# HGRN2 attention and a Serf feed-forward layer: causal masks of seven chunks on ScalarE and GpSimd, a mask before the state's products, and stages of two turns at other slots

## The chip, the cores and the metric

The kernel runs on one NeuronCore of a Trainium2 chip. Its engines work side by side, each with its own in-order queue: TensorE (PE, with its weight loads listed as PEld) does matrix products into PSUM, VectorE (DVE) and ScalarE (ACT) do elementwise work on SBUF and PSUM, GpSimd (POOL) does elementwise work on SBUF, and SyncE (SP) issues nearly all of the DMAs. Semaphores order work between engines. The metric is the device time of one execution in microseconds, as the median of several runs.

## The reference

There are 4 batches, 8 heads, 768 time steps and a head size of 48. The first part is a gated linear recurrence per head, the second a feed-forward layer with the activation h·erf(softplus(h)):

```python
f = 1.0 / (1.0 + np.exp(-f_logit))
for t in range(S):
    state = f[:, :, t, :, None] * state + np.einsum('bhd,bhe->bhde', k[:, :, t], v[:, :, t])
    y[:, :, t] = np.einsum('bhd,bhde->bhe', q[:, :, t], state)
...
x = y.transpose(0, 2, 1, 3).reshape(B * S, H * D)      # 3072 x 384
h = x @ w_in                                           # 384 x 2048
sp = np.maximum(h, 0.0) + np.log1p(np.exp(-np.abs(h)))
out = (h * erf(sp)) @ w_out                            # 2048 x 384
```

## The kernel before

The 3072 rows are cut into 24 chunks of 128 time steps, numbered g = 0 to 23, six to a batch (c = g mod 6). Two chunks make a block of 256 rows; there are twelve blocks.

**Attention, four stages for each chunk.** The recurrence is done in chunks: within a chunk through a masked matrix of scores, across chunks through a state.

- `stage_d(g)`: a matmul with the triangular matrix `tri` sums the logarithms of the decays down the chunk (`ps_d`, L358). ScalarE takes exp of both signs (`dp`, `kd`, L361 and L364). For g >= 3 four small DMAs on SP put the last row of `dp`, the chunk's total decay, into `Tall` (L367). VectorE multiplies q and k by them (`qd`, `kd`, L371 and L375).
- `stage_t(g)`: eight transposes of `qd` and `kd` (`ps_t`, L385), copied out of PSUM as `qT` and `kT` (L391, L393, L395).
- `stage_s(g)`: eight matmuls give the scores `sc` (L414), 128 keys by 8 heads by 128 queries, and VectorE multiplies them by `tri` into `A` (L419): the causal mask. Ahead of the scores stands `state(g)`: eight products `dS` (L433), then four VectorE instructions (`Sn`, `Mbd`, L446 and L449; two L442 in a batch's first chunk) that add the old state and multiply by `Tall`.
- `stage_y(g)`: the products of `A` with v and of `qT` with the state of the chunk before (`y`, L146), which ScalarE copies to `xT` (L462).

`ps_d`, `ps_t`, `dS` and `y` share two PSUM buffers in rotation (`ps_at`), so each of them waits until the one before the last has been read. The scores have one buffer of their own (`ps_sc`); `A` has one in SBUF.

**Feed-forward.** `hidden` computes h for a block in four groups of 12 matmuls (L515), each evicted by ScalarE (L522) from one of two PSUM buffers. `activate` approximates the activation with an Exp, three Tanh and VectorE products (L152, L155, L160, L487, L489), one step at a time. `prepare` clamps the logits of a block on VectorE (L335) and takes Exp and Ln on ScalarE (L339, L340); Exp with Ln and Tanh lie in different tables, so that a change between them is an ACT_TABLE_LOAD. The last product runs through `project_first` for block 0 (L598) and from then on through `project`, which needs seven partial products of half size instead of eight (L645). For it `sum_w` on GpSimd and `sum_h` on VectorE form sums of the weights and of h (L543), and `plus` adds the seven results into the rows of the output in `scratch` (L653, first a copy L661).

**Weights.** w_in and w_out come as 64-bit numbers, in eight pieces each (p0 to p15). Every piece is rounded to 32 bits by one ScalarE pass (L285) and six VectorE passes (L287, L291, L296, L300, L305, L310), at the rate of the counter `due`. A group of `hidden` in the first turn needs its pieces of w_in before it runs.

**Order.** All of it is a schedule written by hand: under `manual_schedule` each engine runs its instructions in the order in which the program emits them. After the first three chunks come turns `it`. A turn runs through slots s, one matmul of the feed-forward part each; at the slots in the list `at` the stages in `todo` are emitted. In turn 0 (96 slots) `at` is written out; in turn 1 (48 slots) it is computed. `prepare(2)` is emitted at slot 17 of turn 0, later ones 14 slots before the `stage_d` that needs them. At each slot the weights' steps come first, then the stage, then `prepare`, then a step of the activation. DMAs are issued by SP in the same order.

Of the kernel before, what the change touches and what calls it, by code (L numbers as in the profile page):

```python
# [45 lines left out]
ALU = mybir.AluOpType  # L46
# [21 lines left out]
P = 128  # L68
# [3 lines left out]
def kernel(  # L72
# [10 lines left out]
    nc = tc.nc  # L83
    B, H, S, D = q.shape
# [8 lines left out]
    NCH = S // P  # L93
# [12 lines left out]
    def fixed(name, shape, dtype=FP32, pool=const):  # L106
        return pool.tile(shape, dtype, name=name)
# [82 lines left out]

    NS, NA = 3, 3
    S_WORDS = NS * NA * FG // 2 * P
    scratch = fixed("scratch", [P, S_WORDS + 7 * DH], pool=fix)
    sums_sb = scratch[:, 0:S_WORDS].rearrange("p (b n j t) -> p b n j t", b=NS, n=NA, j=FG // 2)
    rows_sb = scratch[:, S_WORDS:].rearrange("p (n c) -> p n c", n=7)

    def w_sums(gi):
        return wT[:, gi, :].rearrange("p (n j c) -> p n j c", n=NT, j=FG // 2)
# [197 lines left out]

    def stage_s(g):
        b, c = divmod(g, NCH)
        qT, kT = qTs[g], kTs.pop(g)
        if g in totals:  # L400

            pairs = dps[g % 2][:].rearrange("t (a r) d -> t a (r d)", r=2)
            for a in range(HP):
                nc.tensor.matmul(
                    totals[g][:, a : a + 1], lhsT=pairs[:, a, :], rhs=ident[:, P - 1 : P],
                    start=True, stop=True,
                )
            nc.vector.tensor_copy(out=Tall[:, g, :], in_=totals.pop(g))
        if c < NCH - 1:
            state(g, c)  # L410
        sc = ps_sc.tile([P, 2, HP, P], FP32, name="sc", tag="sc")
        for a in range(HP):
            for r in range(2):
                nc.tensor.matmul(  # L414
                    sc[:, r, a, :], lhsT=kT[rows(r), a, :], rhs=qT[rows(r), a, :],
                    start=True, stop=True,
                )
        A = work1.tile([P, 2, HP, P], FP32, name="A", tag="A")
        nc.vector.tensor_tensor(  # L419
            out=A[:].rearrange("s r a t -> s (r a) t"),  # L420
            in0=sc[:].rearrange("s r a t -> s (r a) t"),
            in1=tri[:].unsqueeze(1).broadcast_to((P, H, P)),
            op=ALU.mult,
        )
        As[g] = A

    def state(g, c):
        dS = ps_at.tile([P, HP, D], FP32, name="dS", tag="at")
# [185 lines left out]
    def project(blk):  # L614


        ops = [ps_moe.tile([P, 2, 512], FP32, name="ops", tag="moe") for _ in range(2)]
        end = blk == n_blocks - 1
        ops.append(ps_sc.tile([P, 2, 512], FP32, name="ops", tag="sc") if end else ops[1])
        place = {n: ops[i][:, j, k * DH : (k + 1) * DH] for n, (i, j, k) in {  # L620
            1: (0, 0, 0), 2: (0, 1, 0), 6: (0, 1, 1), 5: (1, 0, 0), 7: (1, 0, 1), 3: (2, 1, 0), 4: (2, 1, 1),
        }.items()}
        first = [1, 2, 5, 3]

        def pair(n):
            i, j = {2: (0, 1), 5: (1, 0), 3: (2, 1)}[n]
            return ops[i][:, j, 0 : 2 * DH].rearrange("p (n c) -> p n c", n=2)

        def products(gis, ns):
            for gi in gis:  # L630
                gr = groups[blk, gi]
                while gr["sums"] is None:
                    sum_step()
                a11, a12, a21, a22 = blocks(gr["h"])
                w = w_out_sb[:, FG * gi : FG * (gi + 1), :]
                s, t = gr["sums"], w_sums(gi)
                for j in range(2):
                    w1, w2 = w[:, j, :], w[:, 2 + j, :]
                    for n in ns:
                        x, y = {  # L640
                            1: (a11, w1[:, 0:DH]), 2: (a12, w2[:, 0:DH]), 3: (s[2], w2[:, DH:]),
                            4: (a22, t[:, 3, j, :]), 5: (s[0], t[:, 0, j, :]),
                            6: (s[1], t[:, 1, j, :]), 7: (a21, t[:, 2, j, :]),
                        }[n]
                        nc.tensor.matmul(  # L645
                            place[n], lhsT=x[:, j, :], rhs=y,
                            start=(gi == 0 and j == 0 and n in first),
                            stop=(gi == n_g - 1 and j == 1), skip_group_check=True,
                        )
                        yield  # L650

        def plus(out, x, y):
            nc.vector.tensor_tensor(out=out, in0=x, in1=y, op=ALU.add)  # L653

        o = rows_sb
        yield from products((0, 1), (1, 2, 6))
        yield from products((0,), (5, 7, 3, 4))
        to_sum.appendleft(sum_h(groups[blk, 3]))
        yield from products((1,), (5, 7, 3, 4))
        yield from products((2, 3), (1, 2, 6))  # L660
        nc.scalar.copy(out=o[:, 3, :], in_=place[1])  # L661

        plus(o[:, 0:5:4, :], o[:, 3:4, :].broadcast_to((P, 2, DH)), pair(2))
        def fives():

            plus(o[:, 5:7, :], o[:, 4:5, :].broadcast_to((P, 2, DH)), pair(5))

        yield from products((2, 3), (5, 7))
        if end:

            fives()
            plus(o[:, 3, :], o[:, 5, :], place[7])
        yield from products((2, 3), (3, 4))
        if not end:
            fives()
        plus(o[:, 1:3, :], o[:, 5:7, :], pair(3))
        if not end:
            plus(o[:, 3, :], o[:, 5, :], place[7])
        store(blk)

    def chain(*gens):
# [38 lines left out]
    with tc.manual_schedule():  # L720
# [118 lines left out]
        for it in range(n_blocks):  # L839
            gen, n = slots(it)  # L840
            if it == 0:
                todo = [(stage_d, 3), (stage_t, 3), (stage_s, 3), (stage_y, 3), (stage_d, 4), (stage_t, 4),
                        (stage_d, 5), (stage_s, 4), (stage_t, 5), (stage_y, 4)] + stages(2)[4:]
                at = [3, 10, 15, 22, 28, 36, 42, 47, 56, 74, 77, 82, 87, 93]
            else:
                todo = stages(it + 2) if it + 2 < n_blocks else []
                at = [int(3 + (n - 13) / max(1, len(todo)) * i) for i in range(len(todo))]
            if it + 3 < n_blocks:
                prepare_at = at[todo.index((stage_d, (it + 3) * CPB))] - 14
            at, todo = deque(at), deque(todo)  # L850
            for s, _ in enumerate(gen):
                due += (1 if s < 42 else 0.6 if s < 72 else 0.3) if it == 0 else 0.42 if it == 1 else 0.6
                while due >= 1:
                    weights_step()
                    due -= 1
                if s % 6 == 3:
                    load_more()
                if at and s == at[0]:
                    at.popleft()
                    f, g = todo.popleft()  # L860
                    f(g)
                    if f is stage_y:
                        load_to(g + LOOK)
                if it == 0 and s == 17:
                    prepare(2, 0, CPB)
                if it == 0 and s == 9:
                    load_f(6)
                    load_f(7)
                if s == n // 2 and it + 4 < n_blocks:
                    for j in range(CPB):  # L870
                        load_f((it + 4) * CPB + j)
                if it + 3 < n_blocks and s == prepare_at:
                    prepare(it + 3, 0, CPB)
                if it < 2:
                    step = s % 12 == 6 and (it or s >= 24)
                elif it == 2:
                    step = s % 5 in (1, 3)
                else:
                    step = s % 9 in (2, 6)
                if step:  # L880
                    act_step()
                if it == 2:
                    if s == n - 6:
                        to_sum.extend(sum_h(groups[1, gi]) for gi in range(NS))
                    sum_step()
                elif it > 2:
                    if s == n_o and it < n_blocks - 1:
                        to_sum.extend(sum_h(groups[it - 1, gi]) for gi in range(NS))
                    if it == n_blocks - 1 and s % n_o == 40 and s < 2 * n_o:
                        blk = n_blocks - 2 + s // n_o  # L890
                        to_sum.extend(sum_h(groups[blk, gi]) for gi in range(NS))
                    if s < n_o or s % 3 == 0 or it == n_blocks - 1:
                        sum_step()
                if it == n_blocks - 2 and s in (5, 40):
                    next(check)
            assert not todo
# [214 lines left out]
```

## Time and profile before

| what | value |
|---|---|
| median of 3 runs | 629.69 us (629.64 to 629.79) |
| profiled execution, its own time | 629.11 us |
| its span in the profile | 627.4 us |
| TensorE busy | 605.7 us (97%) |
| VectorE busy | 428.1 us (68%) |
| ScalarE busy | 351.8 us (56%) |
| GpSimd busy | 25.6 us (4%) |
| mean granted TensorE clock | 0.992 |

"Span" is the time from the first to the last instruction of one profiled execution. A busy time is the sum of an engine's instructions in it, without those that only branch, wait or issue DMAs. In lists of groups, "idle before" is the engine's idle time ahead of a group, with the instruction that ended most of it. The granted clock is the share of full speed at which TensorE was allowed to run. A timeline has the start in microseconds from the span's beginning, the duration, the engine, the line of the kernel, the operation, the tile written and the tiles read.

### The profile page before, as it was taken

The page shows a single profiled execution, that of the slowest core. Times are in us where ns is not written, and L with a number is a line of the kernel's source. Part 1 is how long each engine was busy: PE and PEld are TensorE (multiplying, and loading weights), DVE is VectorE, ACT ScalarE, POOL GpSimd, SP SyncE. Part 2 cuts the span into 40 slices and gives each one's busy share as a digit, 9 for nine tenths or more (in the row PEclk, how much of TensorE's full clock was granted, in tenths as well). Part 3 has the DMA queues.
Part 4 walks back from the last instruction along what each step waited for, and adds up shares of the span by engine and source line. Part 5 has one row for each costly group of instructions (what it writes and reads, how often), then busy time and mean ns, then how long its engine had stood idle before and what let it go on. Part 6 is the DMA issues. An engine that isn't in the chain of part 4 may idle for free.

```text
span 627.4 us, 11233 instructions
## 1 busy us (share of the span) xinstructions
PE 605.7 (97%) x4727; PEld 536.8 (86%) x4727; DVE 428.1 (68%) x651; ACT 351.8 (56%) x419; POOL 25.6 (4%) x24
## 2 busy tenths in 40 slices
PE   8896899899999999999999999999999999999996
PEld 7775788788668889889889989989989989989995
DVE  4898997755899576667566674684594764756751
ACT  5344655658763666665855856756747446556300
POOL 0000000000491000000000000000000000000000
PEclk9997999999999999999999999999999999999999
DMA  9999623311211211311221131031000000000000
GB/s 197 248 268 256 192 75 64 64 32 21 51 38 27 63 40 25 71 31 26 48 56 25 27 77 25 14 83 31 16 26 1 3 26 0 15 13 0 26 26 30
DMA packets 120633, 37.02 MB, mean 59 GB/s; under 512 B 112384, under 2 KB 115456, under 8 KB 120576
## 3 DMA queue, kind: packets, MB, share of 16 engines
q1 hardware_dynamic: 118496, 35.84, 24.6%
q8 instruction: 39, 0.64, 0.4%
q10 hardware_dynamic: 2080, 0.39, 0.4%
q14 instruction: 18, 0.15, 0.1%
HBM read 31.46 MB, written 4.72 MB: 58 GB/s over the span
## 4 chain that ended last, share of the span: by engine, by line
PE 80%; DVE 9%; ACT 6%; DMA 2%; issue 1%; SPq 1%; POOL 0%; DVEq 0%; POOLq 0%; ACTq 0%
PE hps L515 34%; PE ops L645 31%; PE y L146 5%; PE sc L414 3%; PE ps_t L385 3%; PE ps_d L358 2%; ACT x L155 1%; DVE e L160 1%; DMA Tall<-dp 1%; PE dS L433 1%; DVE scratch L543 1%; DVE A L419 1%; DMA lt<-in_f_logit_dram 1%; PE busy L348 1%; ACT e L152 1%
## 5 line engine op out<-in xcount | busy, mean ns | idle before, releaser
L515 PE MATMUL hps<-xT,w_in_sb 128*128 128x256 f32 x1152 | 262.0, 383 | 1.2 <-ACT xT L462 1.1
L515 PEld LDWEIGHTS hps<-xT,w_in_sb 128*128 128x128 f32 x1152 | 215.9, 191 | 35.4 <-issue 3.0
L160 DVE SCALAR_TENSOR_TENSOR e<-x,e 128x1024 f32<-128x1024 f32 x96 | 120.9, 1259 | 26.5 <-ACT x L155 26.4
L155 ACT ACTIVATE x<-Hg,serf_bias 128x1024 f32<-128x1024 f32 x88 | 97.7, 1142 | 0.1
L645 PE MATMUL ops<-wT,Hg 128*128 128x192 f32 x352 | 86.9, 329 | 0.0
L152 ACT ACTIVATE e<-Hg 128x1024 f32<-128x1024 f32 x44 | 46.6, 1059 | 63.1 <-DVE Hg L489 62.8
L522 ACT COPY Hg<-hps 128x1024 f32<-128x1024 f32 x44 | 44.4, 1010 | 62.5 <-PE hps L515 62.5
L489 DVE TENSOR_TENSOR Hg<-Hg,e 128x1024 f32<-128x1024 f32 x44 | 54.2, 1232 | 32.3 <-ACT e L487 32.3
L645 PE MATMUL ops<-wT,scratch 128*128 128x192 f32 x320 | 75.2, 327 | 0.7 <-DVE scratch L543 0.7
L645 PE MATMUL ops<-w_out_sb,Hg 128*128 128x192 f32 x352 | 74.4, 328 | 0.0
L645 PEld LDWEIGHTS ops<-wT,Hg 128*128 128x128 f32 x352 | 61.8, 190 | 2.7 <-issue 0.2
L645 PEld LDWEIGHTS ops<-w_out_sb,Hg 128*128 128x128 f32 x352 | 60.1, 190 | 3.7 <-issue 1.2
L653 DVE TENSOR_TENSOR scratch<-scratch,ops 128x384 f32<-128x384 f32 (+1 forms) x44 | 21.3, 502 | 53.2 <-ACT scratch L661 44.3
L645 PEld LDWEIGHTS ops<-wT,scratch 128*128 128x128 f32 x320 | 55.9, 190 | 1.0 <-POOL wT L543 1.0
L487 ACT ACTIVATE e<-e 128x1024 f32<-128x1024 f32 x48 | 50.5, 1051 | 6.2 <-DVE e L160 6.2
L371 DVE TENSOR_TENSOR qd<-qn,dp 128x384 f32<-128x384 f32 x24 | 13.4, 558 | 50.4 <-ACT dp L361 50.4
L146 PE MATMUL y<-A,vt 128*32 128x128 f32 x768 | 36.5, 283 | 7.7 <-DVE A L419 6.0
L146 PEld LDWEIGHTS y<-A,vt 128*32 128x32 f32 x768 | 28.1, 111 | 14.8 <-DVE A L419 5.4
L645 PE MATMUL ops<-w_out_sb,scratch 128*128 128x192 f32 x160 | 39.1, 327 | 0.0
L146 PE MATMUL y<-qT,Mbd 128*32 128x128 f32 x480 | 31.2, 280 | 0.0
L419 DVE TENSOR_TENSOR A<-sc,tri 128x1024 f32<-128x1024 f32 x24 | 29.4, 1224 | 2.6 <-PE sc L414 2.1
L462 ACT COPY xT<-y 128x384 f32<-128x384 f32 x24 | 11.3, 472 | 30.5 <-PE y L146 30.5
(108 smaller groups left out, 648.3 us busy)
## 6 DMA issues: line engine op xcount, KB each, us to landing
lt<-in_f_logit_dram SPq DMA_DIRECT2D x24, 192.0 KB, 3.8
qn<-in_q_dram SPq DMA_DIRECT2D x24, 192.0 KB, 4.5
out_dram<-scratch SPq DMA_DIRECT2D x12, 384.0 KB, 3.8
kn<-in_k_dram SPq DMA_DIRECT2D x23, 192.0 KB, 4.0
vt<-in_v_dram SPq DMA_DIRECT2D x23, 192.0 KB, 3.0
w_out_sb<-in_moe_w_in_dram SPq DMA_DIRECT2D x4, 768.0 KB, 6.1
Hg<-in_moe_w_in_dram SPq DMA_DIRECT2D x4, 768.0 KB, 6.8
Hg<-in_moe_w_out_dram SPq DMA_DIRECT2D x4, 768.0 KB, 5.4
```

The lines of the kernel that those rows point to most:

```text
L146: nc.tensor.matmul(y[M * i : M * (i + 1), kt, :], lhsT=terms[n][0], rhs=terms[n][1], start=(n == 0), stop=(n == len(terms) - 1), skip_grou ...
L152: nc.scalar.activation(out=dst[:], in_=h, func=AF.Exp)
L155: nc.scalar.activation(out=dst[:], in_=h, func=AF.Tanh, bias=serf_bias[:, i : i + 1], scale=SERF_KAB[i][0])
L160: nc.vector.scalar_tensor_tensor(out=e[:], in0=x[:], scalar=SERF_KAB[i][2], in1=e[:], op0=ALU.add, op1=ALU.mult)
L385: nc.tensor.transpose(ps[:, a, :], flat[:, a, :], ident[:])
L419: nc.vector.tensor_tensor(out=A[:].rearrange("s r a t -> s (r a) t"), in0=sc[:].rearrange("s r a t -> s (r a) t"), in1=tri[:].unsqueeze(1) ...
L487: nc.scalar.activation(out=e[:], in_=e[:], func=AF.Tanh, scale=SERF_C)
L489: nc.vector.tensor_tensor(out=h, in0=h, in1=e[:], op=ALU.mult)
L515: nc.tensor.matmul(hps[:, j, :], lhsT=w_in_sb[:, kt, ft * P : (ft + 1) * P], rhs=xTs[blk][:, kt, :], start=(kt == 0), stop=(kt == n_k - 1),)
L522: nc.scalar.copy(out=gr["h"], in_=hps[:])
L645: nc.tensor.matmul(place[n], lhsT=x[:, j, :], rhs=y, start=(gi == 0 and j == 0 and n in first), stop=(gi == n_g - 1 and j == 1), skip_grou ...
L653: nc.vector.tensor_tensor(out=out, in0=x, in1=y, op=ALU.add)
```

## The change

It has four parts.

1. **Masks.** For g = 3 to 9 the scores are copied from PSUM to `A` by ScalarE, and GpSimd's `affine_select` then writes zeros in place where the key is later than the query. All other chunks keep VectorE's product with `tri`.
2. **Order within `stage_s`.** For g < 6 `state(g)` is emitted after the mask instead of ahead of the scores' matmuls; this moves the dS products on TensorE and the four instructions on VectorE.
3. **Slots.** The list `at` of turn 0 and the one of turn 1 change, and `prepare(2)` moves from slot 17 to slot 25. As `prepare` of a later block stands 14 slots before its `stage_d`, `prepare(4)` in turn 1 moves from slot 6 to slot 11.
4. **Rows of the output.** `scratch` holds five rows instead of seven: the partial sums `fives` are written over rows 3 and 4 in place of rows 5 and 6, and in the last block the final addition of `place[7]` moves behind that of `pair(3)`.

```diff
-    scratch = fixed("scratch", [P, S_WORDS + 7 * DH], pool=fix)
+    scratch = fixed("scratch", [P, S_WORDS + 5 * DH], pool=fix)
...
     def stage_s(g):
         b, c = divmod(g, NCH)
+        late = g >= 6
...
-        if c < NCH - 1:
+        if late and c < NCH - 1:
             state(g, c)
         sc = ps_sc.tile([P, 2, HP, P], FP32, name="sc", tag="sc")
...
         A = work1.tile([P, 2, HP, P], FP32, name="A", tag="A")
-        nc.vector.tensor_tensor(
-            out=A[:].rearrange("s r a t -> s (r a) t"),
-            in0=sc[:].rearrange("s r a t -> s (r a) t"),
-            in1=tri[:].unsqueeze(1).broadcast_to((P, H, P)),
-            op=ALU.mult,
-        )
+        flat = A[:].rearrange("s r a t -> s (r a) t")
+        if FIRST <= g < 10:
+
+            nc.scalar.copy(out=A[:], in_=sc[:])
+            nc.gpsimd.affine_select(
+                out=flat, in_=flat, pattern=[[0, H], [1, P]], compare_op=ALU.is_ge, fill=0.0,
+                base=0, channel_multiplier=-1,
+            )
+        else:
+            nc.vector.tensor_tensor(
+                out=flat, in0=sc[:].rearrange("s r a t -> s (r a) t"),
+                in1=tri[:].unsqueeze(1).broadcast_to((P, H, P)), op=ALU.mult,
+            )
         As[g] = A
+        if not late and c < NCH - 1:
+            state(g, c)
...
-            plus(o[:, 5:7, :], o[:, 4:5, :].broadcast_to((P, 2, DH)), pair(5))
+            plus(o[:, 3:5, :], o[:, 4:5, :].broadcast_to((P, 2, DH)), pair(5))
...
         if end:
             fives()
-            plus(o[:, 3, :], o[:, 5, :], place[7])
         yield from products((2, 3), (3, 4))
         if not end:
             fives()
-        plus(o[:, 1:3, :], o[:, 5:7, :], pair(3))
-        if not end:
-            plus(o[:, 3, :], o[:, 5, :], place[7])
+        plus(o[:, 1:3, :], o[:, 3:5, :], pair(3))
+        plus(o[:, 3, :], o[:, 3, :], place[7])
         store(blk)
...
-                at = [3, 10, 15, 22, 28, 36, 42, 47, 56, 74, 77, 82, 87, 93]
+                at = [3, 10, 15, 22, 34, 42, 47, 51, 60, 74, 76, 79, 88, 94]
             else:
                 todo = stages(it + 2) if it + 2 < n_blocks else []
-                at = [int(3 + (n - 13) / max(1, len(todo)) * i) for i in range(len(todo))]
+                at = [n * x // 48 for x in (2, 6, 11, 17, 25, 29, 34, 41)] if it == 1 else [int(3 + (n - 13) / max(1, len(todo)) * i) for i in range(len(todo))]
...
-                if it == 0 and s == 17:
+                if it == 0 and s == 25:
                     prepare(2, 0, CPB)
```

More of the change, by code (lines that the diff above doesn't have):

```diff
@@ L192 @@
     S_WORDS = NS * NA * FG // 2 * P
[L193 removed]
+    scratch = fixed("scratch", [P, S_WORDS + 5 * DH], pool=fix)
     sums_sb = scratch[:, 0:S_WORDS].rearrange("p (b n j t) -> p b n j t", b=NS, n=NA, j=FG // 2)
[L195 removed]
+    rows_sb = scratch[:, S_WORDS:].rearrange("p (n c) -> p n c", n=5)
     def w_sums(gi):
```

## The prediction

> **What bounds the kernel now.** I read the chain that ended last first, then the busy time by stretches, then the waits and timelines of the stretches with holes.
>
> ```profile
> PE 80%; DVE 9%; ACT 6%; DMA 2%; issue 1%; SPq 1%; POOL 0%; DVEq 0%; POOLq 0%; ACTq 0%
> ...
> L419 DVE TENSOR_TENSOR A<-sc,tri 128x1024 f32<-128x1024 f32 x24 | 29.4, 1224 | 2.6 <-PE sc L414 2.1
> ```
>
> TensorE (PE) sets the end: it is busy 605.7 of 627.4 us, so an edit on another engine pays only where it closes one of TensorE's holes, 21.7 us in all. The stretches after the start show where they lie (columns after the width: PE, weight loads, DVE, ACT and POOL busy, PE clock, DMA):
>
> ```profile
> 40.00:50.00 10.00, 5.93 (x50) 4.32 (x49) 7.55 (x13) 0.95 (x1) 0.00 (x0) 0.90 1.10 312
> 50.00:60.00 10.00, 7.95 (x75) 6.22 (x76) 9.69 (x14) 5.27 (x8) 0.00 (x0) 0.76 0.94 241
> 60.00:70.00 10.00, 10.00 (x71) 8.49 (x71) 9.72 (x14) 7.86 (x11) 0.00 (x0) 1.00 0.66 224
> 70.00:80.00 10.00, 8.29 (x51) 7.15 (x48) 9.64 (x17) 5.20 (x7) 0.00 (x0) 1.00 0.72 200
> 110.00:120.00 10.00, 8.32 (x90) 6.59 (x88) 5.69 (x10) 7.83 (x11) 0.00 (x0) 1.00 0.13 22
> ```
>
> Holes of 4.1, 2.1, 1.7 and 1.7 us, and a clock of 0.76 behind the first: in finer stretches it is 0.50 from 48 to about 54.8, so the 3.85 us after TensorE's restart at 50.95 do half the work, 1.9 us lost. VectorE (DVE) is full from 50 to 80. Its timeline tells why:
>
> ```profile
> 46.02 0.34 DVE L446 TENSOR_TENSOR Sn<-dS,Mbd 48x192 f32<-48x192 f32 x1
> 48.53 0.35 DVE L449 TENSOR_TENSOR Mbd<-Sn,Tall 48x192 f32<-48x192 f32 x1 [2.16 <-DMA Tall<-dp]
> ...
> 49.67 1.23 DVE L419 TENSOR_TENSOR A<-sc,tri 128x1024 f32<-128x1024 f32 x1
> 50.81 0.95 DVE L305 SCALAR_TENSOR_TENSOR Hg<-Hg 128x768 f32<-128x768 uint32 x1
> ```
>
> The state of g=3 waits for the small DMA of its decays (Tall), which lands at 48.4 behind the weights' loads; the mask L419 stands behind it, and the waits put 5.0 us of TensorE's idle time on that mask ("PE y L146 <- DVE A L419").
>
> **The edits, each against its row.**
>
> *Masks of g=3 to 9.* Seven L419 leave VectorE, 1.14 us each from start to start (49.67 to 50.81). Each becomes a ScalarE (ACT) copy of 128x1024 out of PSUM, 1.01 us by L522, and a GpSimd (POOL) select of 128x1024, which the trace lacks. Its nearest rows:
>
> ```profile
> 0.32 0.10 POOL L1095 MEMSET const-float32-0.0<- 128x1 f32 x1 [0.32 <-issue]
> 0.81 0.20 POOL L735 MEMSET tri<- 128x128 f32 x1 [0.29 <-POOLq L1095]
> 1.09 0.29 POOL L736 TENSOR_SCALAR_AFFINE_SELECT tri<-tri 128x128 f32<-128x128 f32 x1
> ```
>
> From below: the memset's slope, 0.10/127 us an element, gives 0.9 us. From above: the undisturbed sum L543 does 384 elements in 1.02 us, so 2.7 us. I take the select's own row with the memset's fixed 0.10: 0.10 + 1024 x 0.19/128 = 1.6 us. What it costs VectorE is seen where GpSimd works now:
>
> ```profile
> 161.06 1.22 DVE L160 SCALAR_TENSOR_TENSOR e<-x,e 128x1024 f32<-128x1024 f32 x1
> 164.85 2.01 DVE L160 SCALAR_TENSOR_TENSOR e<-x,e 128x1024 f32<-128x1024 f32 x1
> ...
> 164.76 1.02 POOL L543 TENSOR_TENSOR wT<-w_out_sb 128x384 f32<-128x384 f32 x1 [162.86 <-PE ops L598]
> 168.83 2.01 POOL L543 TENSOR_TENSOR wT<-w_out_sb 128x384 f32<-128x384 f32 x1
> ```
>
> An instruction of VectorE that reads SBUF twice took 0.8 us more where GpSimd had begun first. I call d what one select takes from VectorE: nothing if it falls into idle time, 2.7 if all of its longest price is lost; I take the measured 0.8.
>
> The Trainium skill's "SBUF — State Buffer", section "Who interferes with whom", calls the port pair that the two engines share an exclusive lock: whoever starts first blocks the other for a whole instruction. By it d is the whole select when VectorE comes just behind, an estimate of 1.6 from the size above; the row gives half of that, and by the rule each critical select would return more than the 1.14 that its mask saved.
>
> *g=3, TensorE.* Scores end at 41.9 (now ahead of dS), the copy at 43.0, the select by 45.7 even after a VectorE instruction of 1.0. TensorE reaches y(3) at about 46 instead of 50.95. Behind the copy on ScalarE wait two roundings (L285); VectorE wants the first only at 51.5.
>
> *g=3 to 5, what then comes late.* Stages move: `stage_d(4)` from slot 28 to 34, `prepare(2)` from 17 to 25. VectorE is in order, and Tall still lands at 48.4, for SP's order up to there is unchanged. From 49.67: two steps of a piece 1.87, a whole piece 4.65 (53.15 to 57.80), two steps 1.18, then L335 at 57.37 instead of 52.68; the two ScalarE passes (0.87, 0.84) end at 59.7. TensorE, after y(3) (1.7) and 12 products L515 at 0.432 (18 in 7.77 us), is at `ps_d` by 53.4 and waits 6.3 us, then loses 1.9 to the half clock again. So the first hole moves; it doesn't close. On: `ps_d` 0.65, 8 products, 1.9: 65.7. VectorE has qd(4) by 65.5 (57.84 + 3.47 + 3.66 + 0.55). Transposes 0.87, 5 products, `ps_d`, 4 products, scores and dS 1.58, 9 products, the first transposes of g=5: 77.0. The second need dS(4) read: VectorE 64.97 + 0.92 + 0.87 + 4.65 + 2.09 + 0.94 + 1.58 + 1.09 = 77.1. So 77.7 at product 60. Before, product 56 was there at 77.45, product 60 at 79.18. Gain 1.45 - d: **0.65 us**, ends 1.45 and -1.25. Tall(4) now goes behind one more weight load on SP (0.6 us); it is wanted at 76, 13 us after its dp.
>
> *g=0 to 2, mask first.* VectorE used to do the state under the scores' matmuls (27.15 to 28.65) and now waits for the scores: 0.5 us for g=1, 1.0 for g=2. Nothing, because VectorE idles 2.16 for Tall(3); 1.0 to 1.5 if that cover were gone.
>
> *Second turn.* Now ScalarE makes y(6) wait 1.7 us: L339, behind VectorE's L335 at 106.25, then a table load, a Tanh, a rounding, an eviction, and only then the copy qT that frees the PSUM buffer.
>
> ```profile
> 106.83 0.84 ACT L339 ACTIVATE lt<-lt 128x768 f32<-128x768 f32 x1 [2.65 <-DVE lt L335]
> ...
> 112.59 0.59 ACT L391 COPY qT<-ps_t 128x512 f32<-128x512 f32 x1
> ```
>
> The new order puts `prepare(4)` behind qT. From scores at 106.2 (one product sooner): mask copy 1.0, table load 1.3, Tanh 1.15, rounding 0.9, eviction 0.9, qT 0.55 end at 112.0; TensorE with six products behind the transposes arrives at 111.8. **1.7 us** gained, ends 0 and 1.7. Two table loads more (1.28 each) stand before `lt` and `dp(8)`; `lt` is ready at 115.4, `ps_d(8)` comes at about 116: thin cover, under 1 us if it fails.
>
> *Third turn, g=8 and 9.* VectorE and ScalarE alternate on the chain here, and TensorE waits for VectorE 0.7 us at 188 and 0.9 at 197. Two masks save 2 x 1.14, two selects take 2d: +0.7. ScalarE's first copy fits into 3.1 us of idle time before L152, the second pushes a Tanh whose reader came 1.5 us later. GpSimd's sums queue behind the last select, 2 us later than 164.76, and disturb VectorE that much longer. I take **0**, ends +0.7 and 2 x (1.14 - 2.7) = -3.1.
>
> *The end.* `scratch` has five rows, so the last sum of 192 columns follows the last matmul:
>
> ```profile
> 618.80 0.94 DVE L653 TENSOR_TENSOR scratch<-scratch,ops 128x384 f32<-128x384 f32 x2 [1.69 <-PE ops L645]
> 621.40 0.56 DVE L653 TENSOR_TENSOR scratch<-scratch,ops 128x384 f32<-128x384 f32 x1 [1.66 <-PE ops L645]
> ```
>
> 0.94 - 0.56 = 0.38 us, all exposed: **-0.4**. The other blocks' sums lie under matmuls.
>
> Sum: 0.65 + 1.7 + 0 - 0.4 = 1.95 us. The span goes from 627.4 to 625.4; the median lies 2.29 above that span (629.69; the profiled execution's own time is 629.11), so 627.7.
>
> **Rivals.** *A, slower: the select takes VectorE's port.* One mechanism: VectorE full at 70 to 80 and 160 to 190, d = 2.7. Then -1.25 + 1.7 - 3.1 - 0.4 = -3.05: 632.7. With d the balance is (1.45 - d) + 1.7 + 2 x (1.14 - d) - 0.4, zero at d = 1.7. For it: L160's 2.01, and the sums that take 2.0 beside it instead of 1.02. Against it: a select reads once, L543 twice.
>
> *B, the gain is given back.* `lt` and `dp(8)` come late behind the table loads, and the waits at 188 and 197 grow by what TensorE gained: between 139 and 198 the chain runs on VectorE and ScalarE, not on TensorE. Then only the tail is left, 629.7 + 0.4 = 630.1, or the same as before. Against: the chain there begins with TensorE's dS at 138.93 and would move with it.
>
> *C, more.* If VectorE didn't idle for Tall(3), everything after it would be 2.16 earlier: 625.5. Against it: no DMA ahead of Tall moves. That the masks wouldn't leave VectorE at all is excluded: the branch for g=3 to 9 holds no VectorE instruction.
>
> **How the numbers follow.** Forecast 0.43 (its own range 626.2 to 629.1: d from 0 to 1.5 and third turn +0.7 to -0.7), A 0.27, B 0.18, C 0.12. A change under 0.2%, 1.26 us, is what a measurement can't tell from none: 628.4 to 630.9. Of the forecast's 0.43, 0.33 lie below 628.4 and 0.10 above; C is faster; A is slower; of B 0.10 are the same, 0.08 slower. Faster 0.45, same 0.20, slower 0.35. The range reaches from C's 625.4 to 632.2, short of A's worst.
>
> **What would show it.** Right: y(3) starts near 46, `ps_d` of g=4 only near 59.7, with the 0.5 clock now behind 59; selects of about 1.6 us; no wait of y(6) for qT; two sums behind the last matmul. Wrong: selects over 2 us with VectorE's L287 to L310 at twice their 0.56 to 0.96; `ps_d` of g=4 before 57 (then a gain nearer C's); waits over 1.6 us in all for VectorE at 185 to 200.

## The result, and the profile after

The changed kernel took 627.77 us (median of four runs, 627.50 to 629.64), beside 629.74 for the kernel before (four runs, 629.64 to 630.04): a ratio of 0.9974, 95% interval 0.9954 to 0.9994. The forecast was 627.7. The profiled execution took 627.54 us, with a span of 625.8.

The chain that ended last, and the groups of the masks (busy time and mean duration, then idle time before them):

```profile
PE 82%; DVE 8%; ACT 4%; DMA 3%; issue 2%; SPq 1%; DVEq 0%; ACTq 0%
```

```profile
L429 DVE TENSOR_TENSOR A<-sc,tri 128x1024 f32<-128x1024 f32 x17 | 20.8, 1224 | 4.0 <-PE sc L415 3.6
...
L424 POOL TENSOR_SCALAR_AFFINE_SELECT A<-A 128x1024 f32<-128x1024 f32 x7 | 8.8, 1261 | 152.8 <-ACT A L423 152.8
L423 ACT COPY A<-sc 128x1024 f32<-128x1024 f32 x7 | 7.1, 1011 | 7.4 <-PE sc L415 7.1
```

TensorE still sets the end. Seven masks have left VectorE; a select takes 1.26 us on average, and the copy 1.01 as its row had promised. The busy time by stretches, the same ones as before and one more (PE, weight loads, DVE, ACT, POOL busy, PE clock, DMA):

```profile
40.00:50.00 10.00, 10.00 (x116) 7.70 (x115) 9.52 (x15) 4.10 (x6) 1.33 (x1) 1.00 1.10 308
50.00:60.00 10.00, 4.70 (x20) 3.73 (x19) 9.69 (x14) 2.49 (x4) 0.00 (x0) 0.81 1.02 263
60.00:70.00 10.00, 10.00 (x43) 8.12 (x42) 9.69 (x15) 8.35 (x12) 0.00 (x0) 0.85 0.73 250
70.00:80.00 10.00, 9.27 (x72) 7.79 (x71) 9.70 (x16) 6.04 (x9) 1.40 (x1) 1.00 0.48 120
110.00:120.00 10.00, 9.90 (x97) 8.02 (x95) 4.74 (x7) 9.91 (x13) 0.00 (x0) 1.00 0.33 61
120.00:130.00 10.00, 9.79 (x100) 8.16 (x98) 9.77 (x15) 4.72 (x7) 1.09 (x1) 1.00 0.26 47
```

The hole at 40 to 50 is gone, but 50 to 60 now has one of 5.3 us, with a low clock behind it; the 1.7 us at 110 to 120 have shrunk to 0.1, and 0.2 us have appeared at 120 to 130. The waits of TensorE (in all, times, longest) name the new hole:

```profile
PE ps_d L358 <- ACT lt L340: 5.5, 2, 5.3
...
PE ps_t L385 <- DVE Sn L456: 1.9, 3, 1.0
```

The timeline, instructions of all engines in order of time (start, duration, engine, line, what; in brackets the idle time before it and what ended it):

```profile
43.89 1.33 POOL L424 TENSOR_SCALAR_AFFINE_SELECT A<-A 128x1024 f32<-128x1024 f32 x1 [41.99 <-ACT A L423]
44.19 1.45 DVE L287 TENSOR_SCALAR w_in_sb<-w_in_sb 128x768 f32<-128x768 f32 x1
...
48.31 0.35 DVE L459 TENSOR_TENSOR Mbd<-Sn,Tall 48x192 f32<-48x192 f32 x1
...
57.01 0.56 DVE L335 TENSOR_SCALAR lt<-lt 128x768 f32<-128x768 f32 x1
57.60 0.84 ACT L339 ACTIVATE lt<-lt 128x768 f32<-128x768 f32 x1 [7.48 <-DVE lt L335]
59.37 1.65 PE L358 MATMUL ps_d<-lt,tri 128*128 128x384 f32 x2 [5.30 <-ACT lt L340]
...
110.77 0.60 ACT L391 COPY qT<-ps_t 128x512 f32<-128x512 f32 x1
...
121.41 1.09 POOL L424 TENSOR_SCALAR_AFFINE_SELECT A<-A 128x1024 f32<-128x1024 f32 x1 [13.36 <-ACT A L423]
121.75 0.95 DVE L459 TENSOR_TENSOR Mbd<-Sn,Tall 48x192 f32<-48x192 f32 x1
123.23 0.63 PE L385 MATMUL ps_t<-ident,kd 128*128 128x128 f32 x4 [0.21 <-DVE Sn L456]
...
619.16 0.94 DVE L663 TENSOR_TENSOR scratch<-scratch,ops 128x384 f32<-128x384 f32 x2 [2.04 <-PE ops L655]
```

Three readings. First, VectorE's clamp L335 stands at 57.01 in its queue, ScalarE idles 7.48 us for it, and TensorE 5.30. Second, each of the seven VectorE instructions of this profile that start during a select ends only after it: L287 took 1.45 instead of 0.55 us, `Mbd` 0.95 instead of 0.35, and the one at 121.75 ends at 122.70, just behind the select's 122.50. Six of them paid 0.6 to 0.9 us; the seventh starts so near the select's end that it lost nothing. Third, the end has two sums, 0.94 us instead of 0.56.

To compare kernels, the experiments use three milestones: the start of ScalarE's eviction of the first turn's last group (product 96), that of the second turn's last group, and the start of the last 336 products on TensorE. From them come the lengths of the first turn with all before it, of the second turn, and of the part that holds the third (up to those products):

| kernel | first turn ends | second turn | from there to the last 336 | span |
|---|---|---|---|---|
| before | 100.94 | 32.20 | 433.62 | 627.4 |
| changed | 100.12 | 31.27 | 433.13 | 625.8 |

So the change gained 0.82 us in the first turn, 0.93 in the second, 0.49 after it, 2.24 in all, and gave back 0.6 behind the last matmul. Each row is one execution. The second turn and the part after it repeat to 0.1 us where two kernels have the same schedule there. The first turn doesn't: e4, e6 and e11 below have the same schedule up to slot 93 and end it at 100.30, 99.24 and 99.81. So 0.82 us in the first turn is within what single executions differ by.

### The profile page after: what moved, and what is told of

Its sections match the earlier page's. It is cut to its first block, busy times and chain, and to the rows that moved or that the text cites. A ratio compares the mean times of both kernels' runs of the same rounds, so it can differ in the third digit from the quotient of the medians.

```text
span 625.8 us, 11256 instructions
## 1 busy us (share of the span) xinstructions
PE 606.3 (97%) x4727; PEld 535.5 (86%) x4727; DVE 425.5 (68%) x644; ACT 360.9 (58%) x428; POOL 34.5 (6%) x31
## 4 chain that ended last, share of the span: by engine, by line
PE 82%; DVE 8%; ACT 4%; DMA 3%; issue 2%; SPq 1%; DVEq 0%; ACTq 0%
PE hps L525 34%; PE ops L655 31%; PE y L146 5%; PE sc L415 3%; PE ps_t L385 3%; PE ps_d L358 2%; PE ops L608 1%; DMA Tall<-dp 1%; DVE scratch L553 1%; PE dS L443 1%; DMA qn<-in_q_dram 1%; DVE e L160 1%; ACT x L155 1%; PE ps_d L348 1%; DMA lt<-in_f_logit_dram 1%
## 5 line engine op out<-in xcount | busy, mean ns | idle before, releaser
L160 DVE SCALAR_TENSOR_TENSOR e<-x,e 128x1024 f32<-128x1024 f32 x96 | 121.8, 1269 | 27.0 <-ACT x L155 27.0
L146 PE MATMUL y<-A,vt 128*32 128x128 f32 x768 | 35.2, 277 | 0.2
L655 PEld LDWEIGHTS ops<-w_out_sb,scratch 128*128 128x128 f32 x160 | 27.9, 190 | 0.0
```

What stands on the lines that cost most here:

```text
L146: nc.tensor.matmul(y[M * i : M * (i + 1), kt, :], lhsT=terms[n][0], rhs=terms[n][1], start=(n == 0), stop=(n == len(terms) - 1), skip_grou ...
L160: nc.vector.scalar_tensor_tensor(out=e[:], in0=x[:], scalar=SERF_KAB[i][2], in1=e[:], op0=ALU.add, op1=ALU.mult)
L655: nc.tensor.matmul(place[n], lhsT=x[:, j, :], rhs=y, start=(gi == 0 and j == 0 and n in first), stop=(gi == n_g - 1 and j == 1), skip_grou ...
```

## The experiments

Each ran beside the kernel before on the same chip, and ratios are to that. The single executions of a kernel scattered by 0.5 to 4.4 us (before: 628.0 to 631.7), so that a part of 0.5 us in the second turn or after it is read from the milestones, and the whole from the ratio.

| kernel | median, us | before, us | ratio (95%) | first turn ends | second turn | to last 336 | span |
|---|---|---|---|---|---|---|---|
| e1 masks back | 628.81 | 629.41 | 0.9990 (0.9981 to 0.9999) | 100.46 | 30.71 | 433.59 | 626.0 |
| e2 second turn's slots back | 631.90 | 629.41 | 1.0048 (1.0031 to 1.0065) | 100.12 | 35.10 | 433.18 | 629.6 |
| e3 first turn's slots back | 629.30 | 629.41 | 0.9995 (0.9985 to 1.0006) | 102.17 | 31.01 | 433.16 | 627.4 |
| e4 state first | 627.54 | 629.41 | 0.9970 (0.9959 to 0.9980) | 100.30 | 31.28 | 433.17 | 626.0 |
| e5 masks alone | 630.53 | 629.00 | 1.0018 (1.0004 to 1.0031) | 100.62 | 33.19 | 433.18 | 627.7 |
| e6 rows, slot 93, state | 626.73 | 629.00 | 0.9963 (0.9952 to 0.9974) | 99.24 | 31.01 | 433.15 | 624.1 |
| e7 clamp early | 627.85 | 629.00 | 0.9984 (0.9973 to 0.9994) | 100.54 | 31.27 | 433.07 | 626.1 |
| e8 and slower rounding | 628.52 | 629.00 | 0.9991 (0.9978 to 1.0004) | 99.81 | 31.66 | 433.07 | 625.6 |
| e9 and decays on another queue | 618.60 | 629.21 | 0.9833 (0.9816 to 0.9849) | 94.45 | 31.01 | 433.14 | 618.8 |
| e10 before, decays on another queue | 627.79 | 629.21 | 0.9981 (0.9968 to 0.9993) | 98.80 | 32.21 | 433.52 | 625.4 |
| e11 masks of g = 6, 7 back | 626.27 | 629.21 | 0.9956 (0.9939 to 0.9973) | 99.81 | 30.45 | 433.12 | 624.1 |
| e12 loads behind the decays | 616.86 | 628.84 | 0.9810 (0.9796 to 0.9823) | 90.67 | 30.45 | 433.17 | 614.9 |

### Which part brings the gain: e1 to e5

**e1**, the masks back on VectorE:

```diff
-        if FIRST <= g < 10:
+        if False:
```

> The changed kernel, with the masks of g = 3 to 9 back on VectorE (no ScalarE copy, no GpSimd select); slots, order and rows stay as changed. Own theory (most of the gain is the second turn's order, the masks give only the 0.8 us ahead of product 60): 628.0 to 629.0 us, that is 0.3 to 1.2 above the changed kernel's 627.8. Rival M (the masks leaving VectorE are the gain): 629.5 or more. Rival P (a select takes from VectorE about what its mask saved): 627.8 or less.

628.81 us, inside the own theory's band; both rivals fall. Without the masks' move the first turn ends 0.34 us later, the later part is 0.46 longer, but the second turn is 0.56 us *shorter*. So the masks' move is worth -0.56 and +0.46 in the later parts; the +0.34 in the first turn is too small to tell from the scatter. The 0.46 is seen in one wait of TensorE, for VectorE's sums near 188 (before, then changed; e1 has the 0.7 too):

```profile
PE ops L645 <- DVE scratch L543: 0.7, 1, 0.7
```

```profile
PE ops L655 <- DVE scratch L553: 0.2, 1, 0.2
```

**e2**, the second turn's slots as before, and **e3**, the first turn's:

```diff
-                at = [n * x // 48 for x in (2, 6, 11, 17, 25, 29, 34, 41)] if it == 1 else [int(3 + (n - 13) / max(1, len(todo)) * i) for i in range(len(todo))]
+                at = [int(3 + (n - 13) / max(1, len(todo)) * i) for i in range(len(todo))]
```

> The changed kernel with the second turn's slots computed as before (so prepare(4) at slot 6 again); all else as changed. Own theory: y(6) waits 1.7 us for the copy of qT again, so 629.5 us (629.2 to 629.8). Rival M (masks alone): 627.8, with no such wait, because VectorE reaches the clamp of prepare(4) earlier. Rival B (given back later): the wait is back, but TensorE's waits at 185 to 198 shrink by as much, 627.8 to 628.3.

```diff
-                at = [3, 10, 15, 22, 34, 42, 47, 51, 60, 74, 76, 79, 88, 94]
+                at = [3, 10, 15, 22, 28, 36, 42, 47, 56, 74, 77, 82, 87, 93]
...
-                if it == 0 and s == 25:
+                if it == 0 and s == 17:
```

> The changed kernel with the first turn's slots and prepare(2) at slot 17 as before; masks, order within the scores' stage, second turn and rows as changed. Own theory (the hole for Tall(3) only moves; the new slots let y(3) and twelve products run before it): the product 60 no earlier than 78.4, 627.8 to 628.8 us. Rival S (the new slots of the first turn cost time, since the exp that opens the first transposes of g = 4 is put off by a whole weight piece): under 627.5.

Both lost more than was expected. In e2 the second turn is 3.8 us longer than in the changed kernel. The chain of ScalarE is the one of before with a copy of `A` in it (timeline of ScalarE):

```profile
106.27 0.84 ACT L339 ACTIVATE lt<-lt 128x768 f32<-128x768 f32 x1 [2.65 <-DVE lt L335]
...
110.35 0.99 ACT L423 COPY A<-sc 128x1024 f32<-128x1024 f32 x1
111.25 0.89 ACT L285 ACTIVATE w_out_sb<-scratch 128x768 f32<-128x768 f32 x1
112.04 0.99 ACT L532 COPY Hg<-hps 128x1024 f32<-128x1024 f32 x1
112.94 0.59 ACT L391 COPY qT<-ps_t 128x512 f32<-128x512 f32 x1
```

y(6) therefore waited 2.7 us, 1.0 more than the 1.7 of before: the copy's own duration (TensorE's waits, before, then e2):

```profile
PE y L146 <- ACT qT L391: 1.7, 1, 1.7
```

```profile
PE y L146 <- ACT qT L391: 2.7, 1, 2.7
```

The rest is the clock (stretches of e2; the third value from the right is the granted clock, 0.53 and 0.61 behind the wait):

```profile
112.00:114.00 2.00, 0.33 (x13) 0.36 (x17) 1.76 (x3) 2.00 (x4) 0.50 (x1) 1.00 0.00 0
114.00:116.00 2.00, 2.00 (x30) 1.53 (x24) 1.06 (x2) 0.70 (x3) 0.00 (x0) 0.53 0.00 0
116.00:118.00 2.00, 2.00 (x7) 1.59 (x7) 0.00 (x0) 0.83 (x1) 0.00 (x0) 0.61 0.49 98
```

In e3 the select gave y(3) nearly as early as in the changed kernel (TensorE is busy for 9.25 of the 10 us from 40 to 50), but its copy `xT` stands behind `prepare(2)` on ScalarE, which waits for VectorE (timeline of ScalarE):

```profile
52.88 0.84 ACT L339 ACTIVATE lt<-lt 128x768 f32<-128x768 f32 x1 [8.05 <-DVE lt L335]
...
55.32 0.46 ACT L472 COPY xT<-y 128x384 f32<-128x384 f32 x1
```

TensorE waits 6.6 us for that copy. The early mask was worth nothing until `prepare(2)` was moved behind it.

**e4**, the state ahead of the scores:

```diff
-        late = g >= 6
+        late = True
```

> The changed kernel with the state's products ahead of the scores for every chunk, as before; masks, slots and rows as changed. Own theory (where the state stands is hidden by the 5.3 us wait for ps_d of g = 4): 627.5 to 628.2 us. Rival O (with the state ahead, the four VectorE instructions for g = 3 wait for Tall(3) and the mask no longer, but the scores come 0.7 us later on TensorE in each of the first six chunks, and y(0) to y(2) with them): 628.5 or more.

627.54 us: as the own theory had it, and no worse than the changed kernel's 627.77. The order of mask and state is free here.

**e5** is the kernel before with the masks' branch of the change and nothing else:

```diff
-        nc.vector.tensor_tensor(
...
+        if FIRST <= g < 10:
+            nc.scalar.copy(out=A[:], in_=sc[:])
+            nc.gpsimd.affine_select(
...
+        else:
+            nc.vector.tensor_tensor(
```

> The kernel before with the first part alone: masks of g = 3 to 9 by a ScalarE copy and a GpSimd select; order, slots and rows as before. Own theory, from the two runs that put back one turn's slots each (4.1 and 1.5 us above the changed kernel, less the 0.4 of the tail): 632 to 633.6 us, with y(6) waiting about 2.7 us for the copy of qT and the copy of xT for g = 3 behind the exp of prepare(2). Rival M (the masks leaving VectorE are the gain by themselves): 629 or less.

630.53 us, 0.18% slower than before (0.04 to 0.31%). Rival M falls, but so does the sum of 632 or more: e2 and e3 don't add up. y(6) waited 2.7 us here too, as in e2, yet the clock behind it stayed at 1.00 (stretches of e5):

```profile
112.00:114.00 2.00, 0.10 (x4) 0.13 (x8) 1.53 (x3) 2.00 (x4) 0.73 (x1) 1.00 0.00 0
114.00:116.00 2.00, 2.00 (x37) 1.70 (x37) 1.29 (x2) 1.18 (x3) 0.00 (x0) 1.00 0.00 0
```

The profiled execution isn't like most: five of the twelve had a mean granted clock of 0.992 or 0.993 and took 628.48 to 629.63 us, the profiled one among them, and seven had 0.987 to 0.989 and took 630.21 to 631.40. The difference of about 0.003 is what one more stretch of 3.4 us at half clock would make (1.7 of 627 us). So the same wait is followed by a drop in some executions, it seems, and not in others; that the drop of the seven lies behind y(6) isn't shown, as they have no profile. The five are about as fast as the kernel before, and the loss of 0.18% comes from the seven.

So masks alone lose or gain nothing, slots without the masks (e1) gain a little, and the two together gain most.

### Small terms: e6 and e11

**e6** takes e4, puts back the seven rows, and the last stage of the first turn to slot 93:

```diff
-                at = [3, 10, 15, 22, 34, 42, 47, 51, 60, 74, 76, 79, 88, 94]
+                at = [3, 10, 15, 22, 34, 42, 47, 51, 60, 74, 76, 79, 88, 93]
```

> The changed kernel with the state ahead of the scores again, seven rows (last sum of 192 columns under the matmuls) and the last stage of the first turn at slot 93 instead of 94. Own theory: 627.5 of the run with the state ahead, less 0.36 at the end, less 0.35 since two products instead of one lie between y(5) and the first product that needs its copy: 626.8 us (626.4 to 627.2). Rival (both lie beside other waits): 627.3 to 627.8.

626.73 us, as expected, though against e4 the intervals overlap. The profile has both terms: one sum of 0.55 us behind the last matmul instead of 0.94, and the second turn 0.27 us shorter. Between y(5) and the `ps_d` after it, five products take 2.26 us in e6, four 2.08 in the changed kernel: 0.26 us are a wait for the copy of y(5), which only one product covers there. The span is shorter than e4's by more than that (624.1 against 626.0), because this execution's first turn ended 1.06 us sooner, with the same schedule up to slot 93: SP came to the decays of g = 3 at 39.87 instead of 41.21.

**e11** is e6 with two masks back:

```diff
-        if FIRST <= g < 10:
+        if FIRST <= g < 10 and g not in (6, 7):
```

> The run with state first, seven rows and slot 93, with the masks of g = 6 and 7 back on VectorE. Own theory (in the second turn the ScalarE copy and the select cost 0.16 us at y(6) and 0.38 us at the second transposes of g = 8, where an addition of the state's stands beside the select): no wait at 123, 626.2 us (0.5 less than that run's 626.7). Rival M (every mask off VectorE helps): 626.8 or more.

626.27 us, and the second turn 0.56 us shorter, as expected: the masks of g = 6 and 7 on ScalarE and GpSimd cost what e1 had shown. The two spans are equal, 624.1, since this profile's first turn was 0.57 longer (a wait of 6.5 us for `ps_d` of g = 4 instead of 5.3), and against e6 the intervals overlap: the time alone doesn't settle it.

### The hole that moved: e7 to e10 and e12

**e7** takes VectorE's clamp out of `prepare(2)`:

```diff
-                at = [3, 10, 15, 22, 34, 42, 47, 51, 60, 74, 76, 79, 88, 94]
+                at = [3, 10, 15, 22, 30, 42, 47, 51, 60, 74, 76, 79, 88, 94]
...
+                if it == 0 and s == 12:
+                    clamp(2, 0, CPB)
                 if it == 0 and s == 25:
                     prepare(2, 0, CPB)
```

> The changed kernel with VectorE's clamp of prepare(2) at slot 12 and only its two ScalarE passes at slot 25; the sum of g = 4's logarithms at slot 30 instead of 34. Own theory (the wait for ps_d of g = 4 is VectorE's place in its queue, which lags TensorE by 6 us): ps_d starts by 53.5 instead of 59.4, but the transposes of g = 4 then wait for qd, which VectorE reaches at 61 to 62; up to product 60 at most 1.5 us earlier, 626.2 to 627.8 us. Rival H (the late clamp is the whole hole): 5 us less, 622 to 624.

627.85 us, just above what was expected: rival H falls. `ps_d` of g = 4 starts at 52.2, and TensorE then waits at the transposes instead (timeline of TensorE):

```profile
62.43 1.12 PE L389 MATMUL ps_t<-ident,qd 128*128 128x128 f32 x4 [4.21 <-DVE qd L375]
```

**e8** adds a slower counter for the rounding:

```diff
-                due += (1 if s < 42 else 0.6 if s < 72 else 0.3) if it == 0 else 0.42 if it == 1 else 0.6
+                due += (0.8 if s < 72 else 0.3) if it == 0 else 0.45 if it == 1 else 0.6
```

> As the run with the early clamp, and the weights' rounding emitted at 0.8 steps a slot up to slot 72 instead of 1 up to slot 42 and 0.6 up to 72 (0.45 instead of 0.42 in the second turn). Own theory (the rounding stands ahead of the chunks' work on VectorE earlier than a product needs it): transposes of g = 4 at 57 to 59, the second transposes of g = 5 near 72 instead of 77.8, 622 to 625 us. Rival V (VectorE's total work up to there is the bound, the order no matter): 626.5 or more.

628.52 us, where 622 to 625 was expected: rival V's number. But its reason isn't what the timelines show (VectorE, then TensorE, of e8):

```profile
48.50 0.35 DVE L463 TENSOR_TENSOR Mbd<-Sn,Tall 48x192 f32<-48x192 f32 x1 [3.61 <-DMA Tall<-dp]
...
75.76 0.63 PE L389 MATMUL ps_t<-ident,kd 128*128 128x128 f32 x4 [3.44 <-DVE Sn L460]
```

VectorE got rid of its rounding and then stood 3.61 us for the decays of g = 3; later the rounding still stood ahead of the state of g = 4, and TensorE waited 3.44 us for that, with half the clock after it.

**e10** tests the decays by themselves, on the kernel before:

```diff
-                nc.sync.dma_start(
+                (nc.scalar if g == 3 else nc.sync).dma_start(
                     out=Tall[:, g, a : a + 1],
```

> The kernel before, with the four small DMAs of g = 3's decays issued by ScalarE instead of SP, nothing else. Own theory (Tall(3) lands at 48.4 because it goes behind the weights' loads in SP's queue, and VectorE stands 2.16 us for it): it lands before 42, the mask of g = 3 and y(3) come 2.2 us earlier; of it 1.5 to 2.2 us reach the end: 626.8 to 627.5 against 629.0. Rival (the DMA engines are full, whatever the queue): it still lands after 47, 629.0.

627.79 us, a gain of 0.19% (0.07 to 0.32%), just outside the expected band; in the profile, of one of its faster executions, the first turn ends 2.14 us earlier. VectorE no longer stands for the decays, and the mask of g = 3 starts at 47.53 instead of 49.67. Where the delay was is seen on the queues (SP's issues in the kernel before, then ScalarE's in e10):

```profile
38.54 2.64 SPq L266 DMA_DIRECT2D Hg<-in_moe_w_in_dram  x1
41.27 2.65 SPq L367 DMA_DIRECT2D Tall<-dp  x4
```

```profile
34.92 2.51 ACTq L367 DMA_DIRECT2D Tall<-dp  x4
```

`dp` is written by 34.9. SP came to its four issues only at 41.27, for its loads stand ahead of them in order and wait themselves; ScalarE issued them at once. That is 6.35 us. From issue to landing it took 5.2 to 6.6 us there and 4.7 to 5.6 here. So it is SP's queue of issues, and only to a smaller part the transfers under way. The Trainium skill ("DMA: Bandwidth & Descriptors", section "Issuing engines are not separate DMA queues") says that another issuing engine saves no more than sequencer time, usually small. The runs agree on what is saved, not on its size. The price is 2.51 us of ScalarE's own time.

**e9** puts it all together on e6: early clamp, slot 30, the decays on ScalarE's queue, and

```diff
+                due += (0.8 if s < 18 else 0.65 if s < 42 else 0.7 if s < 72 else 0.55) if it == 0 else 0.45 if it == 1 else 0.6
```

> The run with state first, seven rows and slot 93, plus the early clamp, the sum for g = 4 at slot 30, the decays of g = 3 sent by ScalarE's queue instead of SP's, and the weights' rounding at 0.8 steps a slot to slot 18, 0.65 to 42, 0.7 to 72, 0.55 to 96. Own theory (VectorE stood 3.6 us for Tall(3), and rounding ahead of the state of g = 4 held the transposes of g = 5): Tall(3) lands before 42, no wait over 1 us between 40 and 70, second transposes of g = 5 near 70 instead of 77.8; 619 to 623 us. Rival V (VectorE's total is the bound, so the waits only move behind 76): 625 to 627.5.

618.60 us, 1.7% below before and 0.4 us below the own theory's band: rival V falls. TensorE's second transposes of g = 5 start at 72.1 with no wait, 2 us later than expected. One hole is left in the first turn (TensorE, and VectorE, of e9):

```profile
39.40 0.56 DVE L287 TENSOR_SCALAR w_in_sb<-w_in_sb 128x768 f32<-128x768 f32 x1 [1.23 <-ACT w_in_sb L285]
...
45.30 3.32 PE L529 MATMUL hps<-xT,w_in_sb 128*128 128x256 f32 x10 [2.43 <-DVE w_in_sb L310]
```

VectorE waits for ScalarE's first pass over piece p3, which comes behind the DMA issues; TensorE waits 2.43 us for p3. Of this 0.8 us is the select's: p3's last pass, L310 at 43.52, stands beside it and takes 1.72 us instead of 0.96.

**e12** is e9 with the decays on SP again and two loads moved behind them, a rounding that is quicker up to slot 14, the clamp at slot 19, and e11's masks:

```diff
-        load_piece(6)
...
-        load_piece(7)
...
+                due += (0.95 if s < 14 else 0.6 if s < 42 else 0.7 if s < 72 else 0.55) if it == 0 else 0.45 if it == 1 else 0.6
...
+                if it == 0 and s == 4:
+                    load_piece(6)
+                    load_piece(7)
```

> The run with the decays of g = 3 on ScalarE's queue, with four edits: those DMAs on SP again, but the loads of the pieces p6 and p7 issued behind them instead of ahead; rounding at 0.95 steps a slot to slot 14 and 0.6 to 42; the clamp of prepare(2) at slot 19; masks of g = 6 and 7 on VectorE. Own theory (Tall(3) is late only by the two pieces ahead of it, some 3 us each; ScalarE's 0.5 us for each of the four DMAs put p3 off there, which cost a wait of 2.4 us and the half clock behind it): Tall(3) lands near 42 to 43, no wait over 1 us for p3, no clock of 0.5 behind 40; 618.6 - 2.4 - 1.2 - 0.5 = 614.5 us (613.5 to 616.5). Rival (the DMA engines' backlog at 35 is what holds the decays, not these two loads): Tall(3) lands after 46, VectorE stands for it 1 us or more, 617 us or more.

616.86 us, 1.9% below before (1.77 to 2.04%), a third of a microsecond above the band. The profiled span fell by 3.9 us, about as expected (3.78 in the first turn, and the 0.56 of e11's masks in the second); the edits to loads, rounding and clamp weren't tried one by one. But the medians differ by only 1.7, because e9's profiled execution was the slowest of its five (620.53). VectorE reads `Tall` at 45.09 without standing for it, though SP began to issue the four DMAs only at 38.2 and the last one at 42.5, so that 42 to 43 was too early a guess for their landing. No wait for p3 over 0.2 us is left. The stretches:

```profile
40.00:50.00 10.00, 10.00 (x116) 7.70 (x115) 9.70 (x15) 4.68 (x7) 1.30 (x1) 1.00 0.89 244
50.00:60.00 10.00, 10.00 (x50) 8.62 (x49) 9.69 (x15) 7.53 (x11) 0.00 (x0) 1.00 0.95 282
60.00:70.00 10.00, 10.00 (x74) 8.36 (x73) 9.70 (x16) 8.68 (x12) 1.57 (x1) 1.00 1.01 324
70.00:80.00 10.00, 10.00 (x98) 8.12 (x98) 9.72 (x15) 5.99 (x9) 0.00 (x0) 1.00 0.86 197
110.00:120.00 10.00, 10.00 (x104) 8.55 (x101) 9.75 (x14) 2.82 (x5) 0.00 (x0) 1.00 0.29 53
```

TensorE is busy throughout at full clock, and VectorE is as full from 40 to 80 as in the changed kernel, 38.8 us against 38.6. It does the same kind of work there (rounding and the chunks' products) in another order. This version beats both kernels: 616.86 against 627.77 for the changed kernel, each beside a kernel before of 629 to 630.

## Why the prediction was right, and where it was not

**The mechanism held.** TensorE's holes decided, the first hole moved without closing, the wait of y(6) for `qT` went from 1.7 to 0.1 us, and the last sums came out in the open. That the forecast of 627.7 was met to 0.1 us is luck: two terms were wrong by 0.8 and 0.5 us, and the four executions spread from 627.50 to 629.64.

**g = 3.** Predicted: y(3) at about 46, `ps_d` of g = 4 near 59.7, a wait of 6.3 us. Measured: y(3) at 46.7, `ps_d` at 59.37, a wait of 5.3. TensorE came to both 0.7 us later than predicted (54.1 against 53.4 for `ps_d`; the prediction's own terms, 46 + 1.7 + 12 x 0.432, make 52.9). The prediction had put mask-first's 0.5 to 1.0 us on VectorE under the idle time for `Tall`; but ahead of it stand `qd` of g = 3 and piece p2, and TensorE waited 0.7 us for each. In e4, with the state first, 0.2 us of these waits is left and the hole is 6.3 us: what comes earlier there waits longer. "`Tall` still lands at 48.4 and VectorE idles for it" was half wrong: `Mbd` went at 48.31 without waiting. VectorE's own delays had used the idle time up, so that nothing came of it. Nor is 48.4 fixed by SP's order: with the same order ahead of them, SP came to these DMAs at 41.27 in the kernel before, 41.21 in e4, 40.80 in e11 and 39.87 in e6, and in the last two VectorE could read `Tall` at 48.1 and 47.1.

**First turn, 0.65 predicted, 0.82 measured.** The second transposes of g = 5 ended, and product 60 could start, at 78.39 instead of 79.18; predicted were 77.7 and 0.8 for d, 78.5. By the scatter of the first turn (about 1 us) this agrees, but doesn't confirm the term.

**d.** Predicted 0.8 us from VectorE for each select, with 1.6 us for the select. Measured 0.6 to 0.9 in six of the seven cases, nothing in the last, and 1.09 to 1.48 for the select. The prediction weighed this row against the exclusive lock of the Trainium skill ("SBUF — State Buffer", section "Who interferes with whom"). The trace agrees with the lock: each of the six VectorE instructions that lost time ends only when the select has ended. Its d of a whole select, 1.6 by the size then assumed, was still too much: the select is shorter, and VectorE's instruction begins some way into it, 1.04 us at most before its end.

**Second turn, 1.7 predicted, 0.93 measured.** This is the term that was mis-sized. The wait that goes is 1.7 us, as predicted, and e11, with the new slots and none of the side effects, gains 32.20 - 30.45 = 1.75. The side effects were costed at nothing, though the prediction's own sum already left 0.2 us (`qT` done at 112.0, TensorE there at 111.8). Moving the last stage of the first turn from slot 93 to 94 leaves one product for the copy of y(5): 0.26 us. The masks of g = 6 and 7 lengthen the chain on ScalarE and stand beside the state on VectorE: 0.56 us in e1 and again in e11. Beside e11, e6 reaches y(6) 0.16 us later after the transposes, behind the copy of `qT`, and its second transposes of g = 8 come 0.38 us later, behind `Sn`, as `Mbd` ahead of it takes 0.97 instead of 0.35 us beside the select. The prediction had the ScalarE copy in the sum for `qT`, but not what stands behind the select on VectorE in this turn.

**Third turn, 0 predicted, 0.49 measured.** All eleven kernels with g = 8 and 9 off VectorE lie at 433.07 to 433.18, the three others (before, e1, e10) at 433.52 to 433.62. Of the two waits that the prediction named, the one near 188 fell from 0.7 to 0.2 us and the one near 197 stayed (0.9 before, 1.0 now). The select of g = 8 took 0.9 us from an L160 and that of g = 9 nothing, against 2 x 1.14 saved. The 0 was a choice within its range and had no row of its own.

**The end, -0.4 predicted, -0.6 measured.** 0.38 of it is the sum; the rest lies between the last store's issue and the end of the span, 5.7 us against 5.4.

The sum of 1.95 became a span 1.6 us shorter, and the medians differ by 1.97. So errors of -0.8 and +0.5 in two terms cancelled in part, and the scatter did the rest.

**The rivals.** A (the port) needed d = 2.7; d stayed under 1. Its direction is right in the second turn alone. B (given back later) didn't happen: the later part got shorter. C's number was right and its place wrong: getting the decays early is worth 2.14 us in the first turn of the kernel before (e10; 1.4 by the medians), but in the changed kernel VectorE doesn't stand for them.

**What stays open.** The single executions of one kernel differ by up to 4.4 us. Two sources can be seen: when SP comes to the decays (39.87 to 41.27 with the same order), and whether a wait is followed by the half clock (e5). Why SP's loads take differently long wasn't tested. In e7's and e8's ratios this scatter is as large as the effects read from their profiles.

## What to carry to other kernels

When an in-order engine is full, ask what stands ahead of the instruction that someone waits for, not how much work the engine has: e12 gave VectorE as much work from 40 to 80 us as the change did, in another order, and took 10.9 us less, 9.45 of it in the first turn. Moving work to idle engines paid only together with the order that let its result through: alone it lost 0.18%. And a hole that is closed at one place shows the next late thing, one after the other (the clamp, `qd`, the decays, p3), so each trial should be judged by the wait that takes its place before the idea is dropped.

## What the runs showed of the hardware

- The half clock is not a matter of the wait's length alone. Behind a wait of 2.68 us in e2 the granted clock fell to 0.50 for about 3.4 us; behind a wait of 2.68 us at the same place in e5 it stayed at 1.00. In e9, behind 2.43 us, it fell some 1.4 us after TensorE had started again; in the kernel before it fell 2.0 us after TensorE had stopped, in the midst of the wait of 5.0. Up to the last product, each stretch at 0.50 in the fourteen profiles lasted 3.4 or 6.8 us. The Trainium skill ("TensorE: Matmul & The Clock Gate", Part 1 on the clock gate) describes a window of about 3.4 us that runs freely, and a drop after an idle window. That the same wait has both outcomes agrees with a free-running window; that 2.43 us are enough, and 2.0 before, doesn't agree with a whole idle one.
- A GpSimd select over 128x1024 takes 1.09 us at the least. In the changed kernel a VectorE instruction of 0.35 to 0.56 us that fell beside it ended after it, at 0.95 to 1.45 us. `Sn`, which reads one operand from PSUM, was not held: it kept its 0.35 us inside a select in e6, e8 and e9. And the select can be the one that is held up: the one at 85.73 in e9 lasted 4.51 us, while five VectorE instructions ran in their usual times one right behind the other.
- Issuing a DMA of 0.5 KB costs ScalarE 0.5 to 0.6 us each (2.51 for four in e10), and delays whatever is queued there.
